# Fourier mixing and a gated convolution layer: VectorE multiplies the whole gate, in all steps but the last eight

## The chip, the cores and the metric

The kernel runs on one core of a Trainium2 chip. The metric is the device time of one execution in microseconds (us); what is compared is the median over several runs. One execution of each kernel is also recorded by the hardware profiler, and all durations of single instructions come from there.

## The reference, cut to what matters

```python
# x: 8 x 3136 x 256, w_in: 256 x 1024, conv_w: 3 x 1024, w_out: 1024 x 256, all float32
X = np.fft.fft(np.fft.fft(x, axis=1), axis=2).real     # mixing over sequence and features
h = np.maximum(X @ w_in, 0.0)
# convolution over the sequence, three taps for each of the 1024 channels, zero padded
conv = conv_w[0] * h[:, s-1] + conv_w[1] * h[:, s] + conv_w[2] * h[:, s+1]
gate = 1.0 / (1.0 + np.exp(-conv))
out  = (h * gate) @ w_out
```

## The kernel before, in words

The Fourier transform is done with matrix products against tables of sines and cosines. Because the input is real, only half of the frequencies are computed, and the symmetric half follows from sums and differences. For each of the 8 batches the input rows are folded first (the functions in `fold_ops`, lines 157 to 228, on VectorE), then multiplied with the tables into two half spectra `pt` and `qt` (the `Unit`s, whose matmuls go to the PSUM tile `pd`; ScalarE copies one part out, lines 367, 397 and 421, and VectorE adds and subtracts, lines 371 to 434). Rows of the next batch are loaded by plain DMAs and, in mirrored order, by indirect DMAs that GpSimd issues (line 132). The first batches run beside the unpacking of the weights (`narrow`, lines 654 to 677, on VectorE).

The gated layer runs in steps `(b, c, f)`: batch, chunk of frequencies (four in a batch) and block of 128 channels (eight), so 32 steps a batch and 256 in all. A step holds its channels on the 128 partitions and its sequence positions in the free dimension: 770 of them, in the last chunk of a batch 832. Its work is spread over six cycles of one long loop, so that every cycle carries pieces of several steps:

- `seed` (L816, ScalarE) and `products` (TensorE, tiles `pa` and `pb`) make the two halves of `X @ w_in`; `copies` (L837, ScalarE) brings `pb` to SBUF twice, once negated.
- `combine` (L845, VectorE, two operations) adds the halves, clips at zero and writes the tile `h`.
- `first_tap` (L851, ScalarE) writes the scaled first tap into the tile `g`; `middle` (L855) is a DMA issued by GpSimd that adds the middle tap to it; `last_tap` (L860, VectorE) adds the third, three cycles later.
- `sigmoid` (L875, ScalarE), four cycles after the step began, turns `g` into the gate, in two operations on column ranges: first the range that GpSimd is to multiply, then the one that VectorE is to multiply. `shares` gives these ranges: VectorE has the first half `v`, GpSimd the second half `p` and, in the last chunk, the 64 columns `r` that are left over (384 and 448 columns there, 385 and 385 elsewhere).
- `gate` multiplies `g` by `h`: GpSimd its share (L883), VectorE its own (L884).
- `mm2` (TensorE, tile `po`), in the following cycle, multiplies the 128-column pieces of `g` with `w_out` and sums over the eight blocks in PSUM. After the eighth, ScalarE copies the sums out (L908) and DMAs store them. `keep` (L891, ScalarE) first saves the columns `r`, so that two batches share one tile.

The order of instructions on every engine is written out by hand. In each cycle `t` of the loop at line 1083 it is: sigmoid of step t-4, products and copies of t+1, extra work marked "first" and "act", keep of t-5, combine of t, seed of t+2, first tap of t, extra work marked "dve" (one fold, unpacking or spectrum operation as a rule), last tap of t-3, gate of t-4, clearing of the edge columns of the next `h` (`row_of`, L822, GpSimd, only in the first chunk), the middle tap's DMA of t, extra work marked "pool" and "load" (among it the indirect DMAs), mm2 of t-5, extra work marked "pe". Each engine works its instructions in this order and waits at the first that is not ready. All matmuls go through the helper at line 93.

Of the kernel before, what the change touches and what calls it, by code (L numbers as in the profile page):

```python
# [13 lines left out]
ALU = mybir.AluOpType  # L14
# [23 lines left out]
def kernel(  # L38
# [23 lines left out]
    NF = F // P  # L62
# [24 lines left out]
    vt = nc.vector.tensor_tensor  # L87
# [7 lines left out]
    def spare():  # L95

        return pso.tile([P, 2, D], F32, name="po", tag="po").rearrange("p a d -> p (a d)")
# [764 lines left out]
    def shares(s):  # L862


        ch = chunks[s[1]]
        w = ch.w - 2
        n = ch.rest[0] if ch.last else w
        m = n - n // 2
        return slice(0, m), slice(m, n), slice(n, w)

    def sigmoid(s):

        v, p, r = shares(s)
        for c in (slice(p.start, r.stop), v):
            act(gs[s][:, c], gs[s][:, c], AF.Sigmoid, scale=cw[:, 1, s[2]:s[2] + 1])  # L875

    def gate(s):

        b, c, f = s
        g, h = gs[s], hs.pop(s)[:, 1:]  # L880
        v, p, r = shares(s)
        p = slice(p.start, r.stop)
        gt(g[:, p], g[:, p], h[:, p], op=ALU.mult)  # L883
        vt(g[:, v], g[:, v], h[:, v], op=ALU.mult)  # L884
# [83 lines left out]
    for i, u in enumerate(us[j] for j in (4, 2, 3, 7, 8)):  # L968
        u.matmuls(0, 1)
        if i == 0:  # L970
            p = spare()
# [12 lines left out]
    steps = [(b, c, f) for b in range(B) for c in range(len(chunks)) for f in range(NF)]  # L984
# [98 lines left out]
    for t in range(n + LAG):  # L1083
# [3 lines left out]
        if 0 <= t - 4 < n:  # L1087
            sigmoid(steps[t - 4])
# [17 lines left out]
        if 0 <= t - 4 < n:  # L1106
            gate(steps[t - 4])
# [75 lines left out]
```

## Time and profile before

| | |
|---|---|
| median of 3 runs | 1167.69 us (1164.38 to 1167.98) |
| the profiled execution | 1167.47 us, its span 1165.7 us |
| TensorE busy | 1143.1 us, granted clock 0.997 in the mean |
| VectorE busy | 978.5 us |
| ScalarE busy | 943.7 us |
| GpSimd busy | 604.7 us, of it 294.5 in the 256 multiplies of L883 |

PE is TensorE's matmuls, PEld its weight loads, DVE is VectorE, ACT ScalarE and POOL GpSimd. Busy time is the time in which an instruction of the engine was running, whether it worked or was held; idle time is listed with what ended it, as in `[2.02 <-POOL h L822]`: the engine stood for 2.02 us, until GpSimd's work of line 822 on the tile h was done. All places are in us from the start of the span. A matmul in float32 shows as two instructions, so a step has 12 on `po` and 2 each on `pa` and `pb`.

### The profile page before, as it was taken

What the parts mean: (1) busy time and instruction counts of PE and PEld (TensorE: products, weight loads), DVE (VectorE), ACT (ScalarE), POOL (GpSimd) and SP (SyncE); (2) the same over time, 40 slices, a digit from 0 to 9 for tenths busy, and PEclk for the clock granted to TensorE, in tenths of its full rate; (3) what the DMA queues carried; (4) which work ended last, traced back from release to release, by engine and by line L of the source; (5) the groups of instructions that cost most, each with busy time, mean ns of one, the idle gap of its engine ahead of it and who ended that gap; (6) DMA issues with size and microseconds to landing.
All of it is one profiled execution on the core that took longest, in us unless ns stands there. A gap on an engine that the chain in (4) does not pass through costs nothing.

```text
span 1165.7 us, 15936 instructions
## 1 busy us (share of the span) xinstructions
PE 1143.1 (98%) x4834; PEld 892.4 (77%) x4834; DVE 978.5 (84%) x1449; ACT 943.7 (81%) x1950; POOL 604.7 (52%) x741
## 2 busy tenths in 40 slices
PE   6989999999999999999999999999999999999998
PEld 4767787778777777778777777777777787777777
DVE  8799989997887889898877879779787777888885
ACT  3589877888888879887878888888887888898885
POOL 7356545665466464646365464745344444454443
PEclk9899999999999999999999999999999999999999
DMA  9767886777667686757675766865565556666654
GB/s 247 152 111 172 163 149 145 165 164 162 135 142 164 128 192 127 177 112 168 144 173 126 153 132 133 178 130 122 130 130 99 120 122 143 136 127 130 127 115 102
DMA packets 107602, 167.54 MB, mean 144 GB/s; under 512 B 32104, under 2 KB 62838, under 8 KB 107517
## 3 DMA queue, kind: packets, MB, share of 16 engines
q0 software_dynamic: 42160, 115.87, 52.0%
q1 hardware_dynamic: 64616, 50.53, 15.7%
q8 instruction: 38, 0.62, 0.2%
q14 instruction: 47, 0.39, 0.1%
q10 hardware_dynamic: 741, 0.14, 0.1%
HBM read 37.80 MB, written 25.74 MB: 55 GB/s over the span
## 4 chain that ended last, share of the span: by engine, by line
PE 79%; ACT 5%; DVE 4%; issue 2%; DVEq 0%; ACTq 0%
PE po L93 50%; PE pb L93 12%; PE pa L93 12%; PE pd L93 6%; DVE g L860 1%; ACT g L875 1%; ACT nb L837 1%; ACT os L908 1%; ACT pa L816 0%; DVE h L845 0%; ACT g L851 0%; DVE g L884 0%; DVE xh L168 0%; DVE w L194 0%; DVE xh L157 0%
## 5 line engine op out<-in xcount | busy, mean ns | idle before, releaser
L93 PE MATMUL po<-wout,g 128*128 128x256 f32 x3072 | 706.5, 379 | 5.3 <-DVE g L884 4.5
L93 PEld LDWEIGHTS po<-wout,g 128*128 128x128 f32 x3072 | 580.5, 190 | 150.8 <-issue 19.4
L855 POOL DMA_DIRECT2D g<-h x256 | 227.4, 888 | 470.0 <-ACT g L851 293.5
L875 ACT ACTIVATE g<-g,cw 128x385 f32<-128x385 f32 (+2 forms) x512 | 292.3, 625 | 67.2 <-DVE g L860 66.3
L883 POOL TENSOR_TENSOR g<-g,h 128x385 f32<-128x385 f32 (+1 forms) x256 | 294.5, 1151 | 44.5 <-ACT g L875 42.8
L837 ACT ACTIVATE nb<-pb 128x386 f32<-128x386 f32 (+3 forms) x512 | 227.0, 498 | 109.5 <-PE pb L93 108.9
L845 DVE CUSTOM_DVE_ANT_0 h<-pa,nb 128x386 f32<-128x386 f32 (+3 forms) x512 | 264.4, 556 | 28.1 <-POOL h L822 19.0
L860 DVE SCALAR_TENSOR_TENSOR g<-h,cw,g 128x770 f32<-128x770 f32 (+1 forms) x256 | 282.4, 1103 | 0.0
L851 ACT ACTIVATE g<-h,cw 128x770 f32<-128x770 f32 (+1 forms) x256 | 244.4, 955 | 0.0
L93 PE MATMUL pb<-qt,G 127*128 127x387 f32 (+2 forms) x512 | 214.5, 500 | 2.8 <-ACT nb L837 2.4
L93 PE MATMUL pa<-pt,G 128*128 128x387 f32 (+2 forms) x512 | 212.3, 495 | 0.5 <-ACT pa L816 0.5
L884 DVE TENSOR_TENSOR g<-g,h 128x385 f32<-128x385 f32 (+1 forms) x256 | 189.9, 742 | 24.6 <-ACT g L875 24.4
L816 ACT ACTIVATE pa<-eb,ge 128x387 f32<-128x387 f32 (+2 forms) x256 | 155.4, 607 | 1.5 <-DVE h L845 1.2
L93 PEld LDWEIGHTS pa<-pt,G 128*128 128x128 f32 x512 | 97.1, 190 | 74.7 <-issue 18.4
L132 POOL DMA_INDIRECT xh<-in_x_dram,idx x64 | 91.0, 1421 | 20.1 <-issue 11.4
L93 PEld LDWEIGHTS pb<-qt,G 127*128 127x128 f32 x512 | 91.1, 190 | 10.5 <-ACT nb L837 5.0
L93 PE MATMUL pd<-tab,w 98*128 98x197 f32 (+2 forms) x448 | 97.7, 317 | 0.2 <-DVE as L428 0.2
L93 PEld LDWEIGHTS pd<-tab,w 98*128 98x128 f32 (+1 forms) x448 | 81.9, 191 | 9.5 <-ACT pa L816 0.6
L908 ACT COPY os<-po 128x256 f32<-128x256 f32 x196 | 57.3, 393 | 6.5 <-PE po L93 6.5
L157 DVE TENSOR_TENSOR xh<-xh 98x1020 f32<-98x1020 f32 (+1 forms) x32 | 48.2, 1509 | 0.8 <-DMA xh<-in_x_dram,idx 0.7
L168 DVE TENSOR_TENSOR xh<-xh 98x1024 f32<-98x1024 f32 (+1 forms) x32 | 48.5, 1517 | 0.1
L194 DVE TENSOR_TENSOR w<-xh 98x508 f32<-98x508 f32 (+1 forms) x32 | 35.1, 1097 | 0.1
(149 smaller groups left out, 438.8 us busy)
## 6 DMA issues: line engine op xcount, KB each, us to landing
g<-h POOLq DMA_DIRECT2D x192, 385.0 KB, 4.0
g<-h POOLq DMA_DIRECT2D x64, 416.0 KB, 4.1
out_dram<-os SPq DMA_DIRECT2D x96, 256.0 KB
xh<-in_x_dram SPq DMA_DIRECT2D x16, 784.0 KB
eb<-ed SPq DMA_DIRECT2D x16, 193.5 KB
raw<-in_moe_w_in_dram SPq DMA_DIRECT2D x4, 512.0 KB
raw<-in_moe_w_out_dram SPq DMA_DIRECT2D x1, 2048.0 KB
eb<-ed SPq DMA_DIRECT2D x8, 209.0 KB
```

What stands on the lines that cost most here:

```text
L93: nc.tensor.matmul(o, l, r, start=start, stop=stop, skip_group_check=True)
L132: nc.gpsimd.indirect_dma_start(out=xh[b, h][0:NP, 7 - m].rearrange("p q d -> p (q d)"), out_offset=None, in_=bass.AP(tensor=x.tensor, offs ...
L816: act(pa[s][:, 0:n], eb[b, c], AF.Copy, scale=ge[:, f:f + 1])
L837: act(nb[s][:, i, cols], p[:, cols], AF.Copy, scale=-1.0 if i else 1.0)
L845: nc.vector._custom_dve(TENSOR_ADD_SAT, out=to, in0=a[:, cols], in1=c[:, i, cols], s0=BIG, s1=0.0)
L851: act(gs[s], hs[s][:, 0:n], AF.Copy, scale=cw[:, 0, s[2]:s[2] + 1])
L855: nc.gpsimd.dma_start(out=gs[s], in_=hs[s][:, 1:1 + n], accum_op=ALU.add)
L860: stt(out=g, in0=h[:, k:k + n], scalar=cw[:, k, f:f + 1], in1=g, op0=ALU.mult, op1=ALU.add)
L875: act(gs[s][:, c], gs[s][:, c], AF.Sigmoid, scale=cw[:, 1, s[2]:s[2] + 1])
L883: gt(g[:, p], g[:, p], h[:, p], op=ALU.mult)
L884: vt(g[:, v], g[:, v], h[:, v], op=ALU.mult)
L908: nc.scalar.copy(out=osb[:, j % 2], in_=pt[:, j % 2])
```

## The change

In all steps but the last `NF` = 8, the sigmoid is one ScalarE operation over all 770 (or 832) columns, and the multiply is one VectorE operation over all of them; GpSimd has no multiply in these steps. The last eight steps keep the two sigmoids and the shared multiply. Nothing else is moved.

```diff
+    def whole(s):
+
+        return steps.index(s) < len(steps) - NF
+
     def sigmoid(s):
 
         v, p, r = shares(s)
-        for c in (slice(p.start, r.stop), v):
+        for c in [slice(0, r.stop)] if whole(s) else (slice(p.start, r.stop), v):
             act(gs[s][:, c], gs[s][:, c], AF.Sigmoid, scale=cw[:, 1, s[2]:s[2] + 1])
 
     def gate(s):
...
         g, h = gs[s], hs.pop(s)[:, 1:]
         v, p, r = shares(s)
+        if whole(s):
+            vt(g, g, h[:, 0:r.stop], op=ALU.mult)
+            return
         p = slice(p.start, r.stop)
         gt(g[:, p], g[:, p], h[:, p], op=ALU.mult)
         vt(g[:, v], g[:, v], h[:, v], op=ALU.mult)
```

## The prediction

> **What bounds the kernel now.** I read the page first (busy time by engine and the chain of work that ended last), then busy time in stages, and then, inside the stages where TensorE loses time, the groups of instructions of VectorE.
>
> ```profile
> PE 1143.1 (98%) x4834; PEld 892.4 (77%) x4834; DVE 978.5 (84%) x1449; ACT 943.7 (81%) x1950; POOL 604.7 (52%) x741
> ```
>
> ```profile
> PE 79%; ACT 5%; DVE 4%; issue 2%; DVEq 0%; ACTq 0%
> ```
>
> ```profile
> 60.00:139.00 79.00, 74.69 (x306) 54.79 (x305) 78.14 (x113) 68.56 (x153) 46.71 (x60) 1.00 0.73 149
> 180.00:240.00 60.00, 58.66 (x241) 43.30 (x240) 59.20 (x80) 49.05 (x101) 36.67 (x48) 1.00 0.67 145
> 205.00:237.00 32.00, 30.69 (x121) 22.28 (x120) 31.20 (x42) 26.16 (x54) 21.26 (x26) 1.00 0.72 163
> 240.00:1140.00 900.00, 898.49 (x3798) 706.88 (x3797) 745.93 (x1098) 755.78 (x1533) 461.25 (x548) 1.00 0.67 140
> ```
>
> TensorE carries 79% of the chain. In the windows the columns are PE, PEld, DVE, ACT and POOL. From 240 us on TensorE is busy 898.5 of 900 us at a granted clock of 1.00, 898.5 / 3798 = 0.237 us a matmul, and VectorE only 746 of 900 (83%): a change on VectorE, ScalarE or GpSimd can move that stage only where it makes a single step late. Before 240 us it is otherwise. From 60 to 139 us and from 180 to 240 us VectorE is busy 78.1 of 79 and 59.2 of 60 us: there it is the bound, because the fold of the next batches (L157 to L228) and the unpacking of weights (L654 to L669) lie beside the gates. By 0.237 us a matmul TensorE could do its 306 in 72.4 of the 79 us, its 241 in 57.0 of the 60, and its 121 of 205 to 237 us in 28.6 of 32: so 6.6 and 3.0 us are the most that these two stages can give. The change is priced in these two stages by the sum of VectorE's work, and behind 240 us by single late steps.
>
> ```profile
> PEld po L93 <- DVE g L884: 5.9, 7, 2.1
> ...
> PEld po L93 <- DVE g L884: 4.4, 5, 1.2
> ...
> PEld po L93 <- DVE g L884: 7.7, 13, 1.2
> ```
>
> These are one row each from the waits of 60 to 139, of 180 to 240 and of 240 us to the end: the output projection waits for VectorE's half of the gate 7, 5 and 13 times, and it is this instruction that the change makes longer.
>
> **Part 1: the longer multiply.**
>
> ```profile
> L884 DVE TENSOR_TENSOR g<-g,h x256: 541/550/2104, 63.1 to 1152.0; 128x385 f32<-128x385 f32 x96, 128x384 f32<-128x384 f32 x32
> L168 DVE TENSOR_TENSOR xh<-xh x32: 1206/1362/2479, 13.7 to 841.0; 98x1024 f32<-98x1024 f32 x16, 99x1024 f32<-99x1024 f32 x16
> ```
>
> The columns are minimum/median/maximum in ns. No row shows a 770-column product of two SBUF tensors, so I take the line through the two minima: (1206 - 541) / (1024 - 385) = 1.04 ns a column, and 541 + 385 x 1.04 = 942 ns, 0.40 us more than now. (The 832 columns of a batch's last chunk add 0.43.) From above, two of today's operations would be 2 x 541 = 1082 ns (+0.54); from below, the columns cost at least their slope, so a gain is excluded. I take +0.40.
>
> **Part 2: the collisions that go.** GpSimd's half is removed. What it does to VectorE shows here:
>
> ```profile
> 129.86 1.05 POOL L132 DMA_INDIRECT xh<-in_x_dram,idx  x1 [0.30 <-issue]
> ...
> 130.63 2.28 DVE L168 TENSOR_TENSOR xh<-xh 99x1024 f32<-99x1024 f32 x1
> 130.93 0.90 POOL L883 TENSOR_TENSOR g<-g,h 128x385 f32<-128x385 f32 x1
> ```
>
> A fold operation that takes 1.21 us undisturbed takes 2.28. It ends at 132.91, which is 1.08 us behind the end of the GpSimd multiply (131.83): it was held for the last 0.28 us of the indirect DMA and then for the 0.90 us of the multiply. The Trainium skill (SBUF — State Buffer, § SBUF: two separate sides) states that VectorE operations with two SBUF inputs and GpSimd operations share one pair of ports under an exclusive lock, held for a whole instruction. The 1.08 us agree with it.
>
> How much this costs in the two stages follows from the groups of VectorE in each, less their undisturbed durations. First the minima, then 60 to 139 us, then 180 to 240 us:
>
> ```profile
> L195 DVE TENSOR_TENSOR w<-xh x32: 673/675/1911, 15.6 to 861.8; 98x508 f32<-98x508 f32 x16, 99x508 f32<-99x508 f32 x16
> L228 DVE SCALAR_TENSOR_TENSOR w<-w,turn,rt x28: 468/532/1871, 111.9 to 846.3; 98x256 f32<-98x256 f32 x28
> L668 DVE TENSOR_SCALAR left<-raw x7: 407/419/1687, 45.1 to 83.3; 128x512 int32<-128x512 int32 x7
> ```
>
> ```profile
> L884 DVE TENSOR_TENSOR g<-g,h 128x385 f32<-128x385 f32 x18 | 10.6, 588 | 0.3 <-ACT g L875 0.3
> L157 DVE TENSOR_TENSOR xh<-xh 98x1020 f32<-98x1020 f32 (+1 forms) x4 | 6.2, 1545 | 0.0
> L168 DVE TENSOR_TENSOR xh<-xh 98x1024 f32<-98x1024 f32 (+1 forms) x3 | 5.6, 1853 | 0.0
> L662 DVE SCALAR_TENSOR_TENSOR wout<-raw,wout 128x512 int32<-128x512 int32 x4 | 3.8, 956 | 0.0
> L228 DVE SCALAR_TENSOR_TENSOR w<-w,turn,rt 98x256 f32<-98x256 f32 x2 | 3.4, 1722 | 0.0
> L194 DVE TENSOR_TENSOR w<-xh 98x508 f32<-98x508 f32 (+1 forms) x3 | 3.1, 1043 | 0.0
> L668 DVE TENSOR_SCALAR left<-raw 128x512 int32<-128x512 int32 x3 | 3.0, 996 | 0.0
> L195 DVE TENSOR_TENSOR w<-xh 98x508 f32<-98x508 f32 (+1 forms) x3 | 2.7, 898 | 0.0
> L654 DVE TENSOR_SCALAR wout<-raw 128x512 int32<-128x512 int32 x3 | 1.9, 640 | 0.0
> ```
>
> ```profile
> L168 DVE TENSOR_TENSOR xh<-xh 98x1024 f32<-98x1024 f32 (+1 forms) x4 | 7.5, 1884 | 0.0
> L884 DVE TENSOR_TENSOR g<-g,h 128x385 f32<-128x385 f32 (+1 forms) x13 | 7.1, 548 | 0.0
> L194 DVE TENSOR_TENSOR w<-xh 98x508 f32<-98x508 f32 (+1 forms) x3 | 5.4, 1808 | 0.0
> L228 DVE SCALAR_TENSOR_TENSOR w<-w,turn,rt 98x256 f32<-98x256 f32 x4 | 3.9, 1006 | 0.0
> L157 DVE TENSOR_TENSOR xh<-xh 99x1020 f32<-99x1020 f32 x2 | 3.0, 1516 | 0.0
> L845 DVE CUSTOM_DVE_ANT_0 h<-pa,nb 128x385 f32<-128x385 f32 (+3 forms) x28 | 14.3, 551 | 0.8 <-POOL h L822 0.8
> ```
>
> Undisturbed I take 1.21 us for L157 and L168, 0.67 for L194, L195 and (same width) 0.68 for L662, 0.47 for L228, 0.41 for L668 and L654, 0.54 for L884. In the first stage the excess is 1.4 (L157) + 2.0 (L168) + 1.1 (L662) + 2.5 (L228) + 1.1 (L194) + 1.8 (L668) + 0.7 (L195) + 0.7 (L654) + 0.9 (L884) = 12.2 us; in the second 2.7 + 3.4 + 2.0 + 0.6 = 8.7 us, and 0.8 us more in which L845 waited for a memset that stands behind the multiply in GpSimd's queue. Not all of it is the multiply's:
>
> ```profile
> L132 POOL DMA_INDIRECT xh<-in_x_dram,idx x16 | 19.4, 1214 | 4.4 <-issue 3.5 <-PE po L93 0.3 <-ACT nb L837 0.3
> ```
>
> This is the group from 60 to 240 us. Indirect DMAs stay, 16 of them, some 12 in the two stages; at the 0.28 us seen above that is 3.4 us kept, 1.7 in each. The bounds for what goes are nothing and everything.
>
> First stage: 18 gates x 0.40 = +7.2, collisions -(12.2 - 1.7) = -10.5, together **-3.3 us**. Second: 13 x 0.40 = +5.2, collisions and wait -(8.7 + 0.8 - 1.7) = -7.8, together **-2.6 us**. Both lie under the 6.6 and 3.0 us that TensorE can use, so they arrive.
>
> **Part 3: late steps behind 240 us.**
>
> ```profile
> 758.35 1.02 DVE L845 CUSTOM_DVE_ANT_0 h<-pa,nb 128x385 f32<-128x385 f32 x2 [2.02 <-POOL h L822]
> ...
> 909.06 0.36 DVE L427 TENSOR_TENSOR as<-as,pd 128x196 f32<-128x196 f32 x1 [4.52 <-ACT as L421]
> ...
> 911.62 0.55 DVE L884 TENSOR_TENSOR g<-g,h 128x385 f32<-128x385 f32 x1
> ...
> 912.23 0.94 PEld L93 LDWEIGHTS po<-wout,g 128*128 128x128 f32 x5 [0.71 <-DVE g L884]
> ```
>
> VectorE works its queue in order: at 909 us it stood 4.52 us behind ScalarE's copy, and the gate and with it the projection came 0.71 us late. In such a place nothing collides, and the 0.40 us arrive whole at TensorE, less what ScalarE gains in front of its copy:
>
> ```profile
> L875 ACT ACTIVATE g<-g,cw 128x385 f32<-128x385 f32 x384 | 216.8, 619 | 56.9 <-DVE g L860 56.0
> L851 ACT ACTIVATE g<-h,cw 128x770 f32<-128x770 f32 x192 | 180.9, 942 | 0.0
> ```
>
> Two sigmoids of 619 ns become one; the nearest 770-column row takes 942 ns, so 2 x 619 - 942 = 296 ns a step at most, and as consecutive operations overlap I take 0.23. So such a place costs 0.40 - 0.23 = 0.17 us, and 13 places +2.2 us (bounds: 0, where collisions in front of the gate go too, and 13 x 0.40 = +5.2). The place at 758 us is of the other kind: VectorE stood 2.02 us behind the memset that waited for GpSimd's multiply, and that goes; I count it and two more as falling out, which leaves 10 x 0.17 = 1.7, and let the 2.02 us repay one gate's growth, -0.4 (an estimate): **+1.3 us**. Elsewhere VectorE has 17% to spare, which hides both the longer multiply and the shorter sigmoid; without that cover every gate would cost its 0.40 us.
>
> Moved past nothing: GpSimd's queue only loses an instruction ahead of the memset of h and of the issue of the accumulating DMA, so both come no later. The multiply was VectorE's last work of a step and still is; queued behind it is the next step's L845, which feeds ScalarE's first tap. The last eight steps and all ahead of the first gate stay.
>
> Sum: -3.3 - 2.6 + 1.3 = **-4.6 us**. The profiled execution took 1167.47 us, close to the median of 1167.69: 1162.9.
>
> **The rivals.** *Slower: the lock is taken by others.* If VectorE's long fold operations were held mainly by indirect DMAs and small copies on GpSimd, the multiplies would only grow. For it: the row at 129.86 holds VectorE too. Against it: of the 1.18 us there 0.90 is L883. With none of the 12.2 + 8.7 + 0.8 = 21.7 us gone the change costs 7.2 + 5.2 + 2.2 = +14.6 (1182.1); it is 3.5 us slower once less than (14.6 - 3.5) / 21.7 = 51% goes, and I forecast 84%. At 40%: +5.9, 1173.4.
>
> *No change: the gain meets another wait.* ScalarE is busy 68.6 of 79 us in the first stage. If its chain of sigmoid, copies and first tap takes over as VectorE gets shorter, half of the 5.9 us stays out and all 13 places remain: -3.0 + 2.2, 1166.7.
>
> *Descriptors starve.*
>
> ```profile
> L855 POOL DMA_DIRECT2D g<-h x256: 850/876/1002, 53.0 to 1144.2; - x128
> ```
>
> The issue of the accumulating DMA hardly varies, whatever VectorE runs beside it. The indirect DMA is stretched, to 1214 ns in the mean from 1050 undisturbed; held by 0.40 us more in each of 12, the loads and the folds behind them come late, +4.8, and the time is 1167.7. In the same section the Trainium skill warns that GpSimd cannot write DMA descriptors while VectorE holds the port pair, which speaks against a longer VectorE operation; the 850 to 1002 ns show no such hold for the accumulating DMA.
>
> *Faster by more.* If every collision goes and the late places gain as much as they lose, -5.0 in the first stage and the 3.0 that TensorE can use in the second: -8.0, 1159.5.
>
> **How the numbers follow.** The forecast, 1160.5 to 1165.5, has 0.52, more gain 0.12, no change by the other wait 0.15, descriptors 0.07, slower by the lock 0.14. About 0.3%, 3.5 us, is what a measurement of this kernel can tell from no change (its three runs lie 1164.4 to 1168.0); a forecast of -4.6 is 1.1 us beyond that line, so of its 0.52 I count 0.42 as faster and 0.10 as the same. With more gain that is 0.54 faster; same 0.10 + 0.15 + 0.07 = 0.32; slower 0.14. Leaving out a tenth at either end, the range is 1159.0 to 1170.0.
>
> **What would show it.** In the profile after, L884 should read about 942 ns at 770 columns with a maximum near it, L875 about 940, L168, L194 and L228 should stand near their minima, VectorE's sum in the two stages should be smaller, and TensorE should become full, now at about 240 us, some 6 us earlier. The prediction is wrong if L168 keeps means near 1.85 us, if 770 columns cost clearly more than 0.94 us, or if the waits of the projection for L884 behind 240 us number far more than 13.

## The result, and the profile after

The changed kernel takes 1161.66 us in the median of 20 runs, the kernel before 1164.95 us in the median of 20: the ratio is 0.9973, its 95% interval 0.9965 to 0.9981, a gain of 3.3 us. The two profiled executions, 1164.47 and 1167.47 us, differ by 3.0 us. The forecast was -4.6 us, with a range of 1159 to 1170.

The page of the kernel after, its busy times and its chain of work:

```profile
PE 1141.6 (98%) x4834; PEld 893.5 (77%) x4834; DVE 959.8 (83%) x1449; ACT 900.7 (77%) x1702; POOL 379.4 (33%) x493
...
PE 86%; DVE 5%; ACT 4%; POOL 2%; issue 2%; DMA 1%; POOLq 0%; ACTq 0%; DVEq 0%
```

VectorE took over 248 half multiplies and is busy 18.7 us *less* (959.8 for 978.5). TensorE's part of the chain grew from 79% to 86%. The single lines of the kernel after, minimum/median/maximum in ns (the whole multiply is now line 887):

```profile
L887 DVE TENSOR_TENSOR g<-g,h x248: 943/956/1026, 63.3 to 1123.3; 128x770 f32<-128x770 f32 x96, 128x832 f32<-128x832 f32 x28
...
L168 DVE TENSOR_TENSOR xh<-xh x32: 1201/1216/1225, 13.3 to 837.6; 98x1024 f32<-98x1024 f32 x16, 99x1024 f32<-99x1024 f32 x16
L195 DVE TENSOR_TENSOR w<-xh x32: 668/680/800, 15.2 to 858.2; 98x508 f32<-98x508 f32 x16, 99x508 f32<-99x508 f32 x16
L228 DVE SCALAR_TENSOR_TENSOR w<-w,turn,rt x28: 464/476/483, 110.8 to 841.9; 98x256 f32<-98x256 f32 x28
L668 DVE TENSOR_SCALAR left<-raw x7: 416/420/492, 45.3 to 82.0; 128x512 int32<-128x512 int32 x7
```

The multiply costs what the line through two minima said, 943 for 942 ns. The maxima show the rest: L168 went up to 2479 ns before and to 1225 now, L228 to 1871 and now 483. From the first gate to the last eight steps VectorE's fold operations are no longer held at all (the 800 ns of L195 lie at 19 us, ahead of the first gate). The windows of the kernel after:

```profile
60.00:139.00 79.00, 76.46 (x316) 56.77 (x315) 78.21 (x119) 67.22 (x139) 36.98 (x42) 1.00 0.74 152
...
180.00:240.00 60.00, 59.94 (x252) 45.66 (x251) 59.20 (x87) 49.76 (x95) 28.50 (x37) 1.00 0.69 147
205.00:237.00 32.00, 32.00 (x132) 24.74 (x132) 31.20 (x47) 27.38 (x52) 19.23 (x20) 1.00 0.80 177
240.00:1140.00 900.00, 897.61 (x3796) 706.94 (x3795) 732.41 (x1091) 718.12 (x1323) 262.40 (x340) 1.00 0.67 140
```

From 205 to 237 us TensorE now does 132 matmuls in place of 121 and is never idle; from 60 to 139 us it does 316 in place of 306. Behind 240 us nothing is won: 897.6 us busy for 898.5. And the waits of the projection for VectorE's multiply, 60 to 139, 180 to 240 and 240 us to the end:

```profile
PEld po L93 <- DVE g L887: 4.4, 7, 1.7
```

```profile
PEld po L93 <- DVE g L887: 0.7, 1, 0.7
```

```profile
PEld po L93 <- DVE g L887: 10.6, 23, 1.2
```

Before they were 5.9, 4.4 and 7.7 us. So the waits of the second stage went, and those behind 240 us grew, in number and in sum.

**Where the 3.0 us lie.** Because every engine follows one written order, the same matmul can be found in both traces, and its place tells how far ahead the changed kernel is. The rows are the first projection of steps 0 and 40 and the last stretch of TensorE, before and then after:

```profile
64.97 2.32 PE L93 MATMUL po<-wout,g 128*128 128x256 f32 x10
...
244.92 2.32 PE L93 MATMUL po<-wout,g 128*128 128x256 f32 x10
...
1140.20 20.73 PE po L93 x96
```

```profile
64.98 2.32 PE L93 MATMUL po<-wout,g 128*128 128x256 f32 x10
...
240.83 2.54 PE L93 MATMUL po<-wout,g 128*128 128x256 f32 x11
...
1137.20 20.73 PE po L93 x96
```

At step 0 they are level (64.97 and 64.98), at step 40 the changed kernel is 4.1 us ahead, at the end 3.0. So 4.1 us were gained ahead of 245 us and 1.1 lost behind. The runs of every kernel fall into groups some 3 us apart, by the clock granted from 20 to 60 us (1.00, or 0.83 to 0.91, in the traces), which moves step 0 (61 to 69 us) in front of all that the kernels here change, and as the median of a few runs can fall between two groups, the experiments are compared by their traces as well, each counted from its own step 0. Differences from the kernel before in us, minus is gained:

| kernel | step 0 to 18 | 18 to 40 | 40 to 255 | sum | ratio of times, 95% interval |
|---|---|---|---|---|---|
| the change | -2.0 | -2.1 | +1.1 | -3.0 | 0.9973 [0.9965, 0.9981] |
| one sigmoid only | +0.9 | -0.8 | -1.1 | -1.1 | 0.9984 [0.9975, 0.9993] |
| whole multiply only | -2.1 | -1.9 | +2.4 | -1.6 | 0.9984 [0.9975, 0.9994] |
| the change in steps 0 to 39 | -2.0 | -2.1 | +0.1 | -4.0 | 0.9959 [0.9946, 0.9972] |
| the change in steps 40 to 247 | -0.4 | +1.3 | +1.1 | +2.0 | 1.0025 [1.0014, 1.0036] |
| the change in steps 8 to 15 | -0.9 | 0.0 | 0.0 | -0.8 | 0.9991 [0.9981, 1.0001] |
| with an idle GpSimd multiply | +9.2 | +7.4 | +17.2 | +33.7 | 1.0266 [1.0250, 1.0283] |
| with an idle GpSimd memset | -1.8 | -2.1 | +1.0 | -2.9 | 0.9974 [0.9964, 0.9985] |
| late steps left shared | -2.0 | -2.1 | -0.9 | -5.0 | 0.9961 [0.9949, 0.9974] |
| whole to 39, one sigmoid in all | -2.0 | -2.1 | -1.2 | -5.3 | 0.9963 [0.9949, 0.9976] |
| one sigmoid, late steps shared | -2.1 | -2.1 | -2.0 | -6.2 | 0.9956 [0.9940, 0.9971] |

### The profile page after: what moved, and what is told of

It is laid out like the page before. It is cut to its first block, busy times and chain, and to the rows that moved or that the text cites. A ratio compares the mean times of both kernels' runs of the same rounds, so it can differ in the third digit from the quotient of the medians.

```text
span 1162.7 us, 15082 instructions
## 1 busy us (share of the span) xinstructions
PE 1141.6 (98%) x4834; PEld 893.5 (77%) x4834; DVE 959.8 (83%) x1449; ACT 900.7 (77%) x1702; POOL 379.4 (33%) x493
## 4 chain that ended last, share of the span: by engine, by line
PE 86%; DVE 5%; ACT 4%; POOL 2%; issue 2%; DMA 1%; POOLq 0%; ACTq 0%; DVEq 0%
PE po L93 54%; PE pb L93 13%; PE pa L93 13%; PE pd L93 6%; DVE g L860 1%; DVE g L887 1%; POOL xh L132 1%; ACT os L915 1%; ACT nb L837 1%; DVE h L845 1%; DMA xh<-in_x_dram,idx 1%; ACT g L879 0%; ACT pa L816 0%; ACT g L851 0%; POOL w L179 0%
## 5 line engine op out<-in xcount | busy, mean ns | idle before, releaser
L855 POOL DMA_DIRECT2D g<-h x256 | 219.6, 858 | 729.1 <-ACT g L851 451.4
L879 ACT ACTIVATE g<-g,cw 128x770 f32<-128x770 f32 (+3 forms) x264 | 246.1, 935 | 45.5 <-DVE g L860 44.1
L860 DVE SCALAR_TENSOR_TENSOR g<-h,cw,g 128x770 f32<-128x770 f32 (+1 forms) x256 | 265.5, 1037 | 0.0
L887 DVE TENSOR_TENSOR g<-g,h 128x770 f32<-128x770 f32 (+1 forms) x248 | 240.3, 969 | 22.3 <-ACT g L879 22.1
L132 POOL DMA_INDIRECT xh<-in_x_dram,idx x64 | 99.5, 1554 | 20.1 <-issue 12.4
L401 DVE TENSOR_TENSOR as<-as,pd 128x196 f32<-128x196 f32 x14 | 5.0, 358 | 46.1 <-ACT as L397 46.1
L179 POOL COPY w<-xh 98x4 f32<-98x4 f32 (+1 forms) x32 | 38.1, 1190 | 3.7 <-DVE xh L173 2.5
L157 DVE TENSOR_TENSOR xh<-xh 98x1020 f32<-98x1020 f32 (+1 forms) x32 | 38.6, 1210 | 0.5 <-DMA xh<-in_x_dram,idx 0.5
L168 DVE TENSOR_TENSOR xh<-xh 98x1024 f32<-98x1024 f32 (+1 forms) x32 | 38.9, 1215 | 0.1
```

The lines of the kernel that those rows point to most:

```text
L132: nc.gpsimd.indirect_dma_start(out=xh[b, h][0:NP, 7 - m].rearrange("p q d -> p (q d)"), out_offset=None, in_=bass.AP(tensor=x.tensor, offs ...
L168: vt(flat(to, to + 2), flat(0, 2), flat(2, 4), op=op)
L855: nc.gpsimd.dma_start(out=gs[s], in_=hs[s][:, 1:1 + n], accum_op=ALU.add)
L860: stt(out=g, in0=h[:, k:k + n], scalar=cw[:, k, f:f + 1], in1=g, op0=ALU.mult, op1=ALU.add)
L887: vt(g, g, h[:, 0:r.stop], op=ALU.mult)
```

## The experiments

**The two parts apart.** In the first kernel only the sigmoid is changed:

```diff
         v, p, r = shares(s)
-        if whole(s):
-            vt(g, g, h[:, 0:r.stop], op=ALU.mult)
-            return
         p = slice(p.start, r.stop)
```

> One sigmoid in all steps but the last eight, the multiply still shared by GpSimd and VectorE. Theory (collisions): the gain of the change comes from GpSimd's multiply no longer holding VectorE, so here the collisions stay: L168 keeps a mean near 1.5 us in the stages before 240 us, and only ScalarE's 0.23 us a step come in, at the places where VectorE waits for ScalarE's copy (six or so behind 240 us): 0.5 to 1.5 us faster than the kernel before. Rival (ScalarE): the shorter sigmoid is what pays, since ScalarE's chain of sigmoid, copies and first tap paces the stages before 240 us: then this alone gives the whole 3 us.

1163.34 us against 1165.06: 1.7 us faster by the medians, 1.1 by the traces, a little over the forecast's upper end by the first and inside it by the second. Nothing of it lies ahead of step 40 in sum. The collisions stayed, as expected: L168 still goes up to 2482 ns, with a mean of 1964 from 60 to 240 us, more than the 1.5 us named. The rival, that the sigmoid gives it all, falls.

In the second only the multiply is changed:

```diff
-        for c in [slice(0, r.stop)] if whole(s) else (slice(p.start, r.stop), v):
+        for c in (slice(p.start, r.stop), v):
```

> VectorE multiplies the whole gate, the sigmoid stays two operations on the two column ranges. Theory (collisions): the stages before 240 us gain nearly all of their 4 us, and the late places behind 240 us lose the whole 0.40 us each in place of 0.2, about ten of them: in sum 0 to 1.5 us faster than the kernel before. Rival (ScalarE): no gain anywhere, and the late places lose, so 2 to 4 us slower than before.

1163.32 us, 1.7 faster by the medians. The collisions are gone (L168 takes at most 1227 ns). The table shows the two halves of it: -4.0 ahead of step 40, +2.4 behind. The multiply gains all that is gained early and costs more behind than the whole change does.

What happens behind 240 us can be read at one step, 193, in four kernels: how long its projection's weight load waited. The kernel before has `[0.71 <-DVE g L884]` in the prediction's row at 912 us. After the change, with one sigmoid only and with the whole multiply only it reads:

```profile
909.01 2.46 PEld L93 LDWEIGHTS po<-wout,g 128*128 128x128 f32 x12 [0.93 <-DVE g L887]
```

```profile
908.47 2.46 PEld L93 LDWEIGHTS po<-wout,g 128*128 128x128 f32 x12 [0.54 <-DVE g L888]
```

```profile
914.25 2.46 PEld L93 LDWEIGHTS po<-wout,g 128*128 128x128 f32 x12 [1.11 <-DVE g L887]
```

The long multiply adds 0.40 us (1.11 - 0.71), the short sigmoid in front of ScalarE's copy takes 0.17 off (0.71 - 0.54), and both together leave +0.22 (0.93).

**The two stretches apart.** The change in steps 0 to 39 alone, and in steps 40 to 247 alone:

```diff
-        return steps.index(s) < len(steps) - NF
+        return steps.index(s) < 40
```

> The change in steps 0 to 39 alone (up to about 240 us), the shared multiply and the two sigmoids behind. Theory (collisions in the stages where VectorE is full): the gain is all there, 3.5 to 4.5 us faster than the kernel before, which is about 1 us better than the whole change, as the late places keep their short multiply. Rival (the gain is spread over all steps, by GpSimd's shorter queue and ScalarE's shorter work): 40 of 248 steps give a sixth of it, about 0.5 us.

```diff
-        return steps.index(s) < len(steps) - NF
+        return 40 <= steps.index(s) < len(steps) - NF
```

> The change in steps 40 to 247 alone, the kernel before up to there. Theory (collisions in the full stages): nothing is gained up to 240 us, and behind it the late places cost about 1 us: 0.5 to 1.5 us slower than the kernel before. Rival (gain spread over all steps): 208 of 248 steps give five sixths, about 2.5 us faster.

The first is 4.3 us faster than the kernel before (1160.72 to 1165.06), the second 2.4 us slower (1167.45). The sign turns where the theory put it. The second is slower than expected: by its trace it loses the expected 1.1 us behind step 40, and 0.9 us ahead of it, where its instructions are those of the kernel before. That loss lies in one place, 1.3 us between steps 18 and 19; why that place ran longer is not settled.

**What holds VectorE.** GpSimd gets a multiply back that does nothing:

```diff
+    junk = const.tile([P, 448], F32, name="junk")
...
-    rp = ctx.enter_context(tc.tile_pool(name="rp", bufs=2))
+    rp = ctx.enter_context(tc.tile_pool(name="rp", bufs=1))
...
         if whole(s):
+            m = r.stop - p.start
+            gt(junk[:, 0:m], h[:, p.start:r.stop], h[:, p.start:r.stop], op=ALU.mult)
             vt(g, g, h[:, 0:r.stop], op=ALU.mult)
             return
```

> The changed kernel with a GpSimd multiply put back at its old place in GpSimd's queue; it squares the second half of h into a scratch tile that nobody reads, so no result hangs on it and nothing waits for it (the buffers of the tile rt are one in place of two, to make room). Theory (GpSimd's multiply holds VectorE): the long multiply stays and the collisions come back, so L168 has a mean near 1.8 us again before 240 us, VectorE needs about 12 us more in the two full stages, and the time is 4 to 10 us over the changed kernel, 1 to 7 us over the kernel before. Rival (nothing but the shorter sigmoid and the lack of a wait on GpSimd's result pay): the same time as the changed kernel, 3 us under the kernel before.

1196.53 us: 31.5 us over the kernel before, far over the upper end of what I expected. The direction is the theory's; the size is not, and the sign named ahead did not come: from 60 to 240 us L168 has a mean of 1.28 us and not 1.8. The groups of VectorE in it (lines moved by one or more by the inserted code, so L861 is the last tap and L890 the multiply) and its fold operation:

```profile
L861 DVE SCALAR_TENSOR_TENSOR g<-h,cw,g 128x770 f32<-128x770 f32 (+1 forms) x256 | 321.5, 1256 | 0.0
L890 DVE TENSOR_TENSOR g<-g,h 128x770 f32<-128x770 f32 (+1 forms) x248 | 264.7, 1067 | 2.0 <-ACT g L880 2.0
```

```profile
L168 DVE TENSOR_TENSOR xh<-xh x32: 1207/1217/2692, 13.4 to 871.1; 98x1024 f32<-98x1024 f32 x16, 99x1024 f32<-99x1024 f32 x16
```

The idle multiply waits for no sigmoid, so it runs earlier in the cycle than the old one and hits the last tap: its mean went from 1037 ns after the change to 1256, that of the multiply from 969 to 1067. L168 is held again, though in fewer of its 32 (its median stays 1217). So this kernel meets its collisions at other instructions than the kernel before. That a GpSimd multiply on whose result nothing hangs makes VectorE's operations longer is shown (VectorE is busy 1067.8 us, after the change 959.8). The 31.5 us are not shown to be all of that kind: the idle multiply is itself held, up to 3.71 us, it has 9.2% of the chain of work from 60 to 260 us, and ScalarE waits there 13.3 us for the memset of L181 that stands behind it in GpSimd's queue. The two costs were not taken apart.

The same with `nc.gpsimd.memset(junk[:, 0:m], 0.0)` in place of the multiply:

> As the dummy multiply, but a GpSimd memset of the same scratch columns: GpSimd writes as many elements and reads none. If any GpSimd operation on SBUF holds VectorE: L168 is stretched, by the memset's own duration (shorter than the multiply's), and the time is 2 to 5 us over the changed kernel. If only GpSimd operations that read SBUF do: L168 stays at 1.21 us, the memset is what is stretched, and the time is that of the changed kernel within 1 us, about 3 us under the kernel before.

1161.93 us, ratio 0.9974: the time of the changed kernel. VectorE's fold operation and, below it, the memset itself:

```profile
L168 DVE TENSOR_TENSOR xh<-xh x32: 1204/1215/1224, 13.2 to 834.8; 98x1024 f32<-98x1024 f32 x16, 99x1024 f32<-99x1024 f32 x16
```

```profile
L889 POOL MEMSET junk<- x248: 410/735/3413, 59.2 to 1120.4; 128x385 f32 x96, 128x448 f32 x28
```

The memset, which reads nothing, holds none of the fold's operations (L168 at most 1224 ns), and it stands in the place of the idle multiply, with the same single buffer of `rt`. The other half of the expectation, that the memset is what gets stretched, does not hold. Only two of the 248 take over 839 ns, and these stand behind a small GpSimd copy that is held:

```profile
236.80 3.19 POOL L179 COPY w<-xh 99x4 f32<-99x4 f32 x1
236.93 3.10 POOL L181 MEMSET w<- 99x4 f32 x1
236.97 3.41 POOL L889 MEMSET junk<- 128x385 f32 x1
```

The others take as long with a VectorE operation of two SBUF inputs beside them as without one (in the median 735 and 731 ns, those of 385 columns).

**Repairing the late steps.** The change without the ten steps at which the projection waits behind 240 us:

```diff
-        return steps.index(s) < len(steps) - NF
+        i = steps.index(s)
+        return i < len(steps) - NF and i not in (71, 83, 99, 113, 129, 145, 161, 177, 193, 209)
```

> The changed kernel, but the ten steps whose projection waits for VectorE's multiply behind 240 us (71, 83, 99, 113, 129, 145, 161, 177, 193, 209) keep the shared multiply and two sigmoids. Theory (the change loses 1 us at these steps, where VectorE comes late from its wait for ScalarE's copy): 0.8 to 1.5 us faster than the changed kernel, 3.8 to 4.8 us faster than the kernel before, as fast as the change in the first 40 steps alone. Rival (the loss behind 240 us is spread over many steps): ten of 208 steps give nothing, 3 us faster than before.

1160.04 us, 5.0 us under the kernel before. Behind step 40 the loss of 1.1 turned into a gain of 0.9: ten steps carried 2.0 us. That is by the trace 0.5 us more than I expected at most; the whole multiplies that remain win something too, where VectorE's wait for GpSimd's memset (the 2.02 us at 758 us) is gone.

Whole multiplies up to step 39 and one sigmoid everywhere (in `gate`, `if whole(s):` becomes `if steps.index(s) < 40:`):

> VectorE multiplies the whole gate in steps 0 to 39 and its half behind; one sigmoid in all steps but the last eight. Theory (the two parts add up stage by stage): the multiply gives its 4.1 us before 240 us, the sigmoid its 1.1 us at the late places behind, and the long multiply costs nothing there: 4.8 to 5.6 us faster than the kernel before, the fastest of all. Rival (the two sigmoids do not matter once the multiply is short): as the change in the first 40 steps alone, 4.0 to 4.4 us faster.

1160.84 us in the median, 4.2 us faster, and 5.3 by the trace (-4.1 ahead of step 40, -1.2 behind): the parts add up by stage in the trace. The median (of eight runs from 1158.95 to 1164.02) misses the theory's 4.8 and lies in the rival's range; the steps behind 40, where the trace gives 1.2 us, speak for the theory. Both remedies together, with the sigmoid left whole at the ten steps (in `gate`, `if whole(s) and steps.index(s) not in (71, ...):`):

> One sigmoid in all steps but the last eight, the multiply whole on VectorE in all steps but the last eight and the ten late ones, where it stays shared. Theory (early collisions, late multiplies and late sigmoids add up): 4.1 us from the steps before 40, 0.9 us from the whole multiplies behind with the late ones left out, and 0.17 us or so from the one sigmoid at each of six late steps: 5.5 to 6.3 us faster than the kernel before, the best of all. Rival (the two late remedies are one and the same): 5.0 us, as with the late steps left as they were.

1160.13 us against 1165.16, 5.0 us faster; 6.2 by the trace, of them 2.0 behind step 40. Its median (eight runs from 1158.50 to 1165.13) is the rival's figure, its trace is in the theory's range: by the traces the one sigmoid adds 1.1 us to the late steps left shared. It is the fastest by its ratio, 0.9956, and faster than both kernels of the case; its interval, 0.9940 to 0.9971, overlaps those of the three kernels at 0.9959 to 0.9963.

**Why the first stage gave so little.**

```diff
-        return steps.index(s) < len(steps) - NF
+        return 8 <= steps.index(s) < 16
```

> The change in steps 8 to 15 alone, whose multiplies the kernel before runs between 98 and 134 us; all other steps as in the kernel before. This asks why the first stage gave less than forecast. By the forecast's rule (VectorE is full, so its work is the time): eight longer multiplies add 3.2 us and collisions of 6.6 us go (L168 1.9, L157 1.2, L228 2.5, L195 0.7, L194 0.3), 3 us or more faster than before. By the other reading (TensorE never waits for L884 in these steps and is itself the bound there): within 0.6 us of the kernel before.

1164.36 us against 1165.16, ratio 0.9991, 0.8 us by the trace as well (the interval of the ratio still takes in 1). It is a little more than 0.6 and far from 3: collisions of 6.6 us went, with 3.2 us of longer multiplies in their place, and nearly nothing of the rest came through to the time, because TensorE was not waiting for VectorE there.

## Why the prediction was right or wrong, point by point

- *The longer multiply, +0.40.* Right: 943 ns at the least, 956 in the median. (For 832 columns the line through the two minima gives 0.47 us more, not the 0.43 in the prediction; they take 1.02 us.)
- *Collisions go, all but 1.7 us in each stage for the indirect DMAs.* The mechanism is right: with the sigmoid alone the collisions stay and nothing is gained ahead of step 40, with the multiply alone they go and all of it is gained, and a memset in the multiply's place brings none back. The remainder was wrong: there is none, and the prediction's row at 129.86 us was misread. This error and that of the first stage partly hid each other: without the 1.7 us it would have read -5.0 for the first stage and the cap of -3.0 for the second, -6.7 in all. In the kernel after, VectorE's fold runs inside an indirect DMA without being held, and a later indirect DMA is what waits:

```profile
94.88 1.08 POOL L132 DMA_INDIRECT xh<-in_x_dram,idx  x1 [0.30 <-issue]
94.97 1.22 DVE L168 TENSOR_TENSOR xh<-xh 98x1024 f32<-98x1024 f32 x1
...
98.86 3.98 POOL L132 DMA_INDIRECT xh<-in_x_dram,idx  x1 [0.30 <-issue]
```

- *First stage, -3.3.* Too much; -2.0 by step 18. The step that failed is "there it is the bound": I took VectorE's 78.1 of 79 us for the proof that its work is the time in the whole stage. A busy VectorE is not a late one. The 7 waits of the projection in that stage lie at its start and its end (69 to 91 us, and 134 to 139 us). From 109 to 134 us, steps 10 to 15, TensorE was never idle in the kernel before, while VectorE was busy 24.66 of 25 us, and the lead of the changed kernel stays at 1.5 us all through:

```profile
109.00:134.00 25.00, 25.00 (x106) 19.00 (x105) 24.66 (x33) 21.38 (x44) 14.26 (x18) 1.00 0.72 152
```

  The kernel with steps 8 to 15 alone gives 0.8 us where the sum says 3.4. The cap of 6.6 us, from a mean of 0.237 us a matmul, did not see it, as it averages over both kinds of steps. The rival "another wait" also has a part here, around 105 us in the kernel after:

```profile
103.70 2.14 POOL L179 COPY w<-xh 98x4 f32<-98x4 f32 x1
...
105.92 0.91 ACT L222 ACTIVATE rt<-w,turn 98x256 f32<-98x256 f32 x2 [1.54 <-POOL w L181]
...
107.35 0.92 PE L93 MATMUL pa<-pt,G 128*128 128x387 f32 x2 [0.30 <-ACT pa L816]
```

  The indirect DMA that took 3.98 us and a GpSimd copy that took 2.14 kept ScalarE waiting 1.54 us, and ScalarE then TensorE 0.30; the lead falls there from 2.1 to 1.5 us, between steps 9 and 10. That this wait would be gone with a faster GpSimd queue was not tried.
- *Second stage, -2.6.* Right: over the stage (steps 25 to 40) the lead grows by 2.3 us; it is 1.4 us at step 33 and 4.1 at step 40. From step 18 to 32 it had shrunk by 0.6, which the sum had not.
- *Late steps, +1.3.* Right in sign; that the size, +1.1, is so near is partly luck. Its two terms: 0.40 us a place as measured at step 193, and 0.17 for the sigmoid where I took 0.23, so a place costs 0.22 and not 0.17. Read step by step, both sides were larger than in the sum: 1.7 us are lost at eight of the ten steps of the repair and 0.5 at step 61, and 1.1 us (not 0.4) are won at steps 83 and 159 to 161. Step 61 is the largest single loss, and no wait for the gate. In the kernel after:

```profile
329.88 3.30 POOL L179 COPY w<-xh 99x4 f32<-99x4 f32 x1
330.00 1.22 DVE L168 TENSOR_TENSOR xh<-xh 99x1024 f32<-99x1024 f32 x1
...
331.14 1.08 DVE L860 SCALAR_TENSOR_TENSOR g<-h,cw,g 128x832 f32<-128x832 f32 x1
...
332.13 1.02 DVE L887 TENSOR_TENSOR g<-g,h 128x832 f32<-128x832 f32 x1
333.26 0.91 ACT L222 ACTIVATE rt<-w,turn 98x256 f32<-98x256 f32 x2 [1.41 <-POOL h L822]
...
334.35 0.30 PEld L93 LDWEIGHTS po<-wout,left 128*128 128x128 f32 x2 [0.64 <-ACT left L898]
```

  GpSimd's small copy takes 0.50 us at this place in the kernel before. Here it ends with VectorE's third operation in a row, at 333.2 us, and ScalarE and TensorE come late behind it. The same 0.5 us stands in the traces of the kernels with the whole multiply only, with the change from step 40 on, and of both that leave the late steps shared; in none of the four without a whole multiply there, and not in the one with the idle memset. So both repairs still carry this loss.
- *The signs of being wrong.* Two of the three stayed away (L168 and the 770 columns). The third came: the projection waits 23 times and not 13 for the gate behind 240 us. The waits that came new are short, 0.16 to 0.35 us, and the loss is the 2.2 us above; the number of waits was no good sign.
- *The sum*: -4.6 forecast, -3.0 between the profiled executions and -3.3 between the medians. Of the 1.6 us between forecast and trace, 1.3 (3.3 - 2.0) is the first stage. That 1161.66 us lies within the forecast's 1160.5 to 1165.5 is partly luck: the 4.6 us were taken off 1167.47, where twenty runs of the kernel before have a median of 1164.95, and 1164.95 - 4.6 = 1160.35 lies just outside.
- *Slower: the lock is taken by others.* Fell: the indirect DMAs hold none of VectorE's fold operations. *Descriptors starve*: the indirect DMAs did get longer, in the mean 1554 ns for 1421 over the whole execution, with the small cost at 105 us.

## What to carry to other kernels

An engine that is busy all the time is only the bound at the steps for which another engine waits: price an edit at those steps, by finding each one's slack between the producer's end and the consumer's start, and not by the sum over a stage. Moving work from GpSimd to VectorE can leave VectorE with less to do, when the GpSimd operation reads SBUF and VectorE's long operations queue up behind it; compare an instruction's maximum with its minimum before trusting its mean. Where an edit gains in one stretch of a program and loses at a few known steps in another, apply it by step.

## What the runs showed of the hardware that was not expected

- Which GpSimd work holds VectorE: a multiply that reads SBUF does (L168 up to 2692 ns with the idle multiply), a memset does not (up to 1224 ns), an indirect DMA does not (1.22 us inside one). The Trainium skill (SBUF — State Buffer, § SBUF: two separate sides) states what fits the first two: a VectorE operation with two SBUF inputs contends only with a GpSimd operation that reads SBUF, and the runs agree. The other way round, VectorE operations of two SBUF inputs in a row hold GpSimd's indirect DMA (967 ns at the least, 3983 at the most after the change) and its copy L179 (3.30 us at step 61, with the third of the row), but not the idle memset (735 and 731 ns with and without them).
- In the kernel before, L168 began at 130.63 us, 0.30 us ahead of GpSimd's multiply (130.93), and was still held to that multiply's end. The same section of the Trainium skill says that whichever starts first keeps the ports for its whole instruction; by the starts that the trace records, this case differs, and the measurement decides. Since the indirect DMA in front of the multiply does not hold VectorE by itself, what held L168 for those 0.30 us stays open. It is no single case: at 139.56 us L168 began 0.49 us ahead of the multiply (140.05 to 140.94) and took 2.48 us, so that it ended 1.10 us behind it.
- L668, an operation of one SBUF input and constants on int32, was held as well (1687 ns before, 492 at most after).
